# Spectral mixing and a gated FFN on one core: inverse tables made on chip, the first batch's mixing on idle PSUM banks, its first norm without memory

## The chip, the cores and the metric

One core of one Trainium2 chip. The time is the device time of one launch in microseconds (us); lower is better. The kernel before takes 1032.24 us (median of 4 runs, 1030.58 to 1034.24).

## The reference, cut to what matters

```python
# x: (8, 3008, 256) fp32; filters: (1505, 256) real and imaginary part
X = np.fft.rfft(x, axis=1)
y = np.fft.irfft(X * (filt_r + 1j * filt_i)[None], n=3008, axis=1)      # mixing along the sequence
t = y.reshape(24064, 256)
tn = t / np.sqrt(np.mean(t * t, -1, keepdims=True) + 1e-6) * rms_g     # RMS norm
g = tn @ w_gate                                                        # 256 -> 1536
out = (g / (1 + np.exp(-g)) * (tn @ w_val)) @ w_out                    # 1536 -> 256
```

## The kernel before

The transform of length 3008 = 47 x 64 is done as matrix products, a batch at a time: a 64-point stage (`a_unit`, table `wa`), a trip through memory that turns the data (`z_store`, `t2_load`), then in 16 units a 47-point stage (`b_unit`, table `wb`), the filter product and the inverse 47-point stage (`bi_unit`, table `wi`), a second trip through memory (`g_store`, `t4_load`), and the inverse 64-point stage (`n_unit`, table `wai`), which already gives the transposed tile that the norm and the FFN want. Every batch has six token tiles, and a tile has 12 FFN slots (`gv`: gate, value, product; `down`: the last product). While the FFN of one batch runs, the mixing and norms of the next are spread over its slots. The first batch has no FFN to hide behind: its mixing is the opening of the program, and this change is about that opening.

```python
psG, psV: 2 PSUM banks each (gate, value)   psO: 2 (output)   psM: 2 (all of mixing and norm)

def a_unit(b, i):                       # 12 a batch
    ps = psM.tile([P, 512], FP32, tag="mx")
    nc.tensor.matmul(ps, wa, x[c][:, 2*r:2*r+2, :])
    nc.scalar.activation(out=t1[c][:, 2*r:2*r+2, :], in_=ps, func=AXT.Copy)
def b_unit(b, i):                       # 16 a batch
    ps = psM.tile([P, 2, D], FP32, tag="mx", name="psb")
    for u in range(2):
        nc.tensor.matmul(ps[:, u, :], wb[:, k, :], t2[k // KC][:, k % KC, :])
    nc.vector.tensor_tensor(out=s1, in0=ps, in1=fr[c][:, r:r+2, :], op=ALU.mult)
    nc.vector.tensor_tensor(out=s2, in0=ps, in1=fi[c][:, r:r+2, :], op=ALU.mult)
def bi_unit(b, i):
    ps = psM.tile([P, 2, D], FP32, tag="mx", name="psi")
    ...                                 # four matmuls with wi on s1, s2; ACT evicts to t3
def t4_load(b, c):                      # four DMAs a chunk, all on the sync queue
    nc.sync.dma_start(t[p0:p0+32], g_d[b, :, r0:r0+XC, :])
def q_unit(b, m):                       # sum of squares by matmul with ones, then rho = u ** -0.5 on POOL
def rho_move(b, m):                     # rho to memory and back, spread over all partitions
    nc.sync.dma_start(r_d[b, m], rho)
    nc.sync.dma_start(rb, r_d[b, m]....partition_broadcast(P))
def xn_unit(b, m):
    nc.gpsimd.tensor_tensor(out=xn, in0=y, in1=rb, op=ALU.mult)
# ... the opening
x_load(0, c) for 4 chunks               # POOL queue
wa, wb, wi[:, 0:8]                      # sync queue
8 fills of the filter tiles on DVE;  filter and FFN weight loads on the POOL queue
12 x a_unit(0), z_store(0);  wi[:, 8:16];  t2_load(0, 0..2);  wi[:, 16:32];  wai, gains
f_dup(0);  16 x (b_unit(0, i), bi_unit(0, i - 1)), f_dup and g_store between
t4_load(0);  norm and rho_move of tiles 0 and 1;  xn_unit(0, 0), xn_unit(0, 1)
x_load(1, c)                            # POOL queue, behind both xn_units
# ... the loop: slot by slot; batch 1's a_units in slots 0 to 11
```

`f_dup(c)` copies a filter tile's lower half to its upper half, one copy on DVE and one on ACT. The line numbers (L...) of the profiles are those of each kernel's own file, so the same step has other numbers before and after.

Of the kernel before, what the change touches and what calls it, by code (L numbers as in the profile page):

```python
# [38 lines left out]
def _make_tables():  # L39
# [19 lines left out]
    wi = np.zeros((P, K2, 2, P))  # L59
    re, im = slice(0, N1), slice(SL, SL + N1)  # L60
    for k2 in range(K2):
        for s in range(48):

            if s < 24:
                k = k2 + 64 * s
                sign, q = 1.0, s
            else:
                j = s - 23
                k = 64 * j - (k2 if k2 else 32)
                sign, q = -1.0, 32 + s - 24  # L70
                if j == 24 and k2:
                    continue
            th = 2 * np.pi * ((n1 * k) % N) / N
            c, sn = np.cos(th), np.sin(th)
            if k == 0 or k == NF - 1:
                sn = np.zeros(N1)
            if k2:
                wb[re, k2, q] = c
                wb[im, k2, q] = sign * sn
                wb[re, k2, HALF + q] = -sn  # L80
                wb[im, k2, HALF + q] = sign * c

                gr = (c, -sn)
                gi = (sign * sn, sign * c)
            else:
                src = re if s < 24 else im
                wb[src, k2, q] = c
                wb[src, k2, HALF + q] = -sn
                m = 1.0 if k in (0, NF - 1) else 2.0
                z = np.zeros(N1)  # L90
                g = (m * c, -m * sn)
                gr, gi = (g, (z, z)) if s < 24 else ((z, z), g)

            wi[q, k2, 0, re] = gr[0]
            wi[q, k2, 0, im] = gi[0]
            wi[HALF + q, k2, 0, re] = gr[1]
            wi[HALF + q, k2, 0, im] = gi[1]
            wi[q, k2, 1, re] = gr[1]
            wi[q, k2, 1, im] = gi[1]
            wi[HALF + q, k2, 1, re] = -gr[0]  # L100
            wi[HALF + q, k2, 1, im] = -gi[0]
    f = np.float16
    wi = wi * S_INV_B
    return (wa.astype(f), (wai * S_INV_A).astype(f), wb.astype(f), wi.astype(f))
# [3 lines left out]
def kernel(  # L108
# [13 lines left out]
    wa_np, wai_np, wb_np, wi_np = _make_tables()  # L122
# [3 lines left out]
    wi_d = nc.inline_tensor(wi_np, name="wi_t").ap()  # L126
# [8 lines left out]
    t1p = ctx.enter_context(tc.tile_pool(name="t1p", bufs=3))  # L135
# [17 lines left out]
    wai = glob.tile([P, P], FP16)  # L153
    wb = glob.tile([KR, K2, P], FP16)
# [25 lines left out]

    def a_unit(b, i):
        c, r = divmod(i, XC // 2)
        if r == 0:
            st[b]["t1"][c] = t1p.tile([P, XC, D], FP16, tag="t1", name="t1")
        ps = psM.tile([P, 512], FP32, tag="mx", name="psa")
        nc.tensor.matmul(ps, wa, st[b]["x"][c][:, 2 * r:2 * r + 2, :], start=True, stop=True)  # L186
        nc.scalar.activation(out=st[b]["t1"][c][:, 2 * r:2 * r + 2, :],
                             in_=ps.rearrange("p (a d) -> p a d", a=2), func=AXT.Copy)
# [14 lines left out]
    def b_unit(b, i):  # L203
        ps = psM.tile([P, 2, D], FP32, tag="mx", name="psb")
# [8 lines left out]
        nc.vector.tensor_tensor(out=s2, in0=ps, in1=fi[c][:, r:r + 2, :], op=ALU.mult)  # L213
        st[b]["s"][i] = (s1, s2)

    def bi_unit(b, i):
        s12 = st[b]["s"].pop(i)
        ps = psM.tile([P, 2, D], FP32, tag="mx", name="psi")
# [13 lines left out]
    def t4_load(b, c):  # L232
        t = t4p.tile([P, XC, D], FP16, tag="t4", name="t4")
        for h in range(2):
            for ri in range(2):
                p0 = h * 64 + ri * 32
                r0 = ri * SL + h * H + c * XC
                nc.sync.dma_start(t[p0:p0 + 32, :, :], g_d[b, :, r0:r0 + XC, :])
        st[b]["t4"][c] = t
# [44 lines left out]
    def rho_move(b, m):  # L284
# [4 lines left out]
        st[b]["u"][m] = rb  # L289

# [88 lines left out]

    with tc.manual_schedule():  # L380
# [3 lines left out]
        nc.sync.dma_start(wb, wb_d)  # L384
        nc.sync.dma_start(wi[:, 0:KC], wi_d[:, 0:KC])
# [3 lines left out]
        nc.vector.memset(ones, 1.0)  # L389
        nc.vector.memset(mhalf, -0.5)  # L390
# [8 lines left out]
        for c in range(NXC):  # L399
            for i in range(3):  # L400
                a_unit(0, 3 * c + i)
            z_store(0, c)
        nc.sync.dma_start(wi[:, KC:2 * KC], wi_d[:, KC:2 * KC])
        for c in range(3):
            t2_load(0, c)
        for c in range(2, NC):
            nc.sync.dma_start(wi[:, c * KC:(c + 1) * KC], wi_d[:, c * KC:(c + 1) * KC])
        nc.sync.dma_start(wai, wai_d)
        for dh in range(2):
            nc.sync.dma_start(gsb[:, dh:dh + 1], moe_rms_g[ds(dh * P, P)].unsqueeze(-1))  # L410
# [14 lines left out]
        for m in range(2):  # L425
            n_unit(0, m, 0)
            n_unit(0, m, 1)
            q_unit(0, m)
            rho_move(0, m)
        for m in range(2):  # L430
            xn_unit(0, m)
# [15 lines left out]

        for m in range(2, 6):
            norm_plan(0, m, (m - 2) * 10)
        for b in range(1, B):  # L450
            t = (b - 1) * 72
            for i in range(12):
                at(t + i, a_unit, b, i)
                if i % 3 == 2:
                    at(t + i + 1, z_store, b, i // 3)
            for c in range(4):
                at(t + 13 + c if c < 3 else t + 24, t2_load, b, c)
            for i in range(16):
                s0 = t + 16 + 2 * i
# [7 lines left out]
            for c in range(4):  # L467
                at(t + 53, t4_load, b, c)
# [45 lines left out]
```

## Time and profile before

| stretch of the opening | us |
|---|---|
| start to the first filter product | 46.5 |
| first product to last inverse eviction (the B stage) | 37.7 |
| last eviction to the first gate matmul | 19.2 |
| first gate matmul, at | 103.4 |
| PE waiting for batch 1's x after that | 6.0 |

First the page: the span in 40 slices of 26 us, the busy share of TensorE and of the DMA engines in tenths.

```profile
PE   2162789999999999999999999999999999999997
DMA  9973556324743356323643356324743343322111
```

TensorE is busy from the fifth slice on; before that it is not. The opening is the only place where much can be won. The timeline of the opening in the kernel before (columns: start, duration, engine, line, operation, output<-inputs, shapes, count; in brackets how long the engine had been idle and what ended that):

```profile
23.72 1.70 SPq L196 DMA_DIRECT2D z_tmp<-t_235  x4
33.64 0.32 SPq L200 DMA_DIRECT2D t_250<-z_tmp  x1
45.88 1.01 PE L207 MATMUL psb<-t_250,wb 96*128 96x256 f16 x4 [22.83 <-DMA t_250<-z_tmp]
46.51 0.69 DVE L212 TENSOR_TENSOR s_266<-psb,fr_113 128x512 f16<-128x512 f32 x1 [25.82 <-PE psb L207]
...
80.40 0.59 PE L207 MATMUL psb<-t_328,wb 96*128 96x256 f16 x2 [0.68 <-ACT t_458 L226]
81.02 0.69 DVE L212 TENSOR_TENSOR s_477<-psb,fr_116 128x512 f16<-128x512 f32 x1 [0.83 <-PE psb L207]
...
83.61 0.59 ACT L226 ACTIVATE t_486<-psi 96x512 f16<-96x512 f32 x1 [1.10 <-PE psi L221]
90.30 1.04 PE L252 MATMUL psn<-wai,t_495 128*128 128x128 f16 x8 [6.72 <-DMA t_500<-g_tmp]
100.51 2.85 POOL L299 TENSOR_TENSOR xn<-y,rb 128x1024 f16<-128x1024 f32 x1 [2.51 <-DMA rb<-r_tmp]
103.41 1.01 PE L319 MATMUL pg<-xn,wg 128*128 128x512 f16 x2 [6.70 <-POOL xn L299]
111.72 0.59 PE L186 MATMUL psa<-xc,wa 128*128 128x512 f16 x1 [6.01 <-DMA xc<-in_x_dram]
```

Read it from above. The turned data of the first stage (t2) lands only at 45.9 us; the last store that it depends on went out at 23.7. In the B stage PE waits for an ACT eviction before it may start the next `psb`, and DVE then waits for that `psb`: two PSUM banks pass between the two kinds of product. The scale goes through memory before POOL may multiply at 100.5. And six of the microseconds after the first gate are a wait for x.

The matmuls of one `psi` start 0.21 us apart in the B stage, and 0.11 us apart in the loop: TensorE works at half its later speed in the B stage.

### The profile page before, as it was taken

The page shows a single profiled execution, that of the slowest core. Times are in us where ns is not written, and L with a number is a line of the kernel's source. Part 1 is how long each engine was busy: PE and PEld are TensorE (multiplying, and loading weights), DVE is VectorE, ACT ScalarE, POOL GpSimd, SP SyncE. Part 2 cuts the span into 40 slices and gives each one's busy share as a digit, 9 for nine tenths or more (in the row PEclk, how much of TensorE's full clock was granted, in tenths as well). Part 3 has the DMA queues.
Part 4 walks back from the last instruction along what each step waited for, and adds up shares of the span by engine and source line. Part 5 has one row for each costly group of instructions (what it writes and reads, how often), then busy time and mean ns, then how long its engine had stood idle before and what let it go on. Part 6 is the DMA issues. An engine that isn't in the chain of part 4 may idle for free.

```text
span 1031.0 us, 17242 instructions
## 1 busy us (share of the span) xinstructions
PE 931.7 (90%) x6240; PEld 565.0 (55%) x6240; DVE 591.7 (57%) x966; ACT 597.5 (58%) x1046; POOL 246.0 (24%) x218
## 2 busy tenths in 40 slices
PE   2162789999999999999999999999999999999997
PEld 0031356655666556655666566655666556656654
DVE  5161257744775457744775467644775467645553
ACT  3043555557655766557655766557655766556543
POOL 5501423113410333013410333013410332023200
PEclk9999999999999999999999999999999999999999
DMA  9973556324743356323643356324743343322111
GB/s 210 192 149 99 112 117 130 91 80 109 156 91 99 79 130 146 99 74 102 159 92 99 78 132 147 102 71 106 156 96 105 80 118 92 99 69 60 41 42 39
DMA packets 95941, 109.51 MB, mean 106 GB/s; under 512 B 17352, under 2 KB 70088, under 8 KB 95568
## 3 DMA queue, kind: packets, MB, share of 16 engines
q1 hardware_dynamic: 85744, 90.64, 33.9%
q0 software_dynamic: 10112, 17.77, 11.2%
q8 instruction: 49, 0.80, 0.3%
q14 instruction: 36, 0.29, 0.1%
HBM read 73.14 MB, written 49.91 MB: 119 GB/s over the span
## 4 chain that ended last, share of the span: by engine, by line
PE 76%; DMA 9%; DVE 5%; ACT 5%; issue 3%; SPq 1%; POOL 0%; ACTq 0%; DVEq 0%; POOLq 0%
PE pg L319 21%; PE pv L319 20%; PE psi L221 6%; PE psb L207 3%; ACT sq L261 2%; PE psn L252 1%; PE psa L186 1%; DMA fi_120<-in_filt_i_dram 1%; DMA fi_119<-in_filt_i_dram 1%; PE psq L269 1%; ACT y L259 1%; DVE hh L324 1%; DMA rb<-r_tmp 1%; DMA fr_114<-in_filt_r_dram 1%; SPq L196 1%
## 5 line engine op out<-in xcount | busy, mean ns | idle before, releaser
L324 DVE TENSOR_TENSOR hh<-pv,sg 128x512 f16<-128x512 f32 (+1 forms) x576 | 390.9, 679 | 363.8 <-ACT sg L323 217.0
L323 ACT ACTIVATE sg<-pg 128x512 f16<-128x512 f32 (+1 forms) x576 | 340.6, 591 | 313.5 <-PE pg L319 311.6
L319 PE MATMUL pg<-xn,wg 128*128 128x512 f16 (+1 forms) x1152 | 340.4, 377 | 6.7 <-POOL xn L299 6.7
L319 PE MATMUL pv<-xn,wv 128*128 128x512 f16 (+1 forms) x1152 | 339.4, 376 | 0.0
L336 PEld LDWEIGHTS <-hh 128*128 128x128 f16 (+1 forms) x2304 | 221.9, 98 | 108.9 <-issue 32.7
L299 POOL TENSOR_TENSOR xn<-y,rb 128x1024 f16<-128x1024 f32 (+1 forms) x48 | 132.5, 2760 | 316.6 <-DMA rb<-r_tmp 233.2
L319 PEld LDWEIGHTS <-wv 128*128 128x128 f16 x1152 | 113.2, 98 | 132.3 <-issue 2.5
L281 POOL TENSOR_TENSOR rho<-u,mhalf 128x4 f32<-128x4 f32 x48 | 48.7, 1015 | 388.1 <-DVE u L279 366.4
L319 PEld LDWEIGHTS <-wg 128*128 128x128 f16 x1152 | 105.9, 98 | 29.0 <-issue 7.3
L221 PEld LDWEIGHTS <-wi 128*128 128x128 f16 x512 | 51.5, 103 | 47.4 <-issue 4.5
L259 ACT ACTIVATE y<-psn,gsb 128x512 f32<-128x512 f32 (+1 forms) x96 | 65.8, 685 | 14.2 <-DMA t_500<-g_tmp 6.7
L186 PE MATMUL psa<-xc,wa 128*128 128x512 f16 x96 | 39.0, 412 | 23.6 <-DMA xc<-in_x_dram 16.6
L207 PEld LDWEIGHTS <-wb 96*128 96x128 f16 x256 | 23.7, 101 | 65.4 <-issue 40.6
L261 ACT ACTIVATE sq<-psn 128x512 f16<-128x512 f32 (+1 forms) x96 | 56.8, 592 | 0.0
L178 POOL DMA_DIRECT2D xc<-in_x_dram x64 | 34.7, 559 | 0.8 <-POOLq L498 0.8
L186 PEld LDWEIGHTS <-wa 128*128 128x128 f16 x96 | 9.5, 100 | 33.8 <-issue 20.4
L269 PEld LDWEIGHTS <-sq 128*128 128x128 f16 (+1 forms) x384 | 17.4, 97 | 14.4 <-ACT sq L261 4.1
L207 PE MATMUL psb<-t_250,wb 96*128 96x256 f16 x8 | 2.3, 410 | 22.9 <-DMA t_250<-z_tmp 22.8
L269 PE MATMUL psq<-ones,sq 128*128 128x1 f16 (+1 forms) x384 | 17.6, 165 | 3.4 <-ACT sq L261 3.4
L279 DVE TENSOR_SCALAR u<-psq 128x4 f32<-128x4 f32 (+2 forms) x56 | 7.8, 152 | 15.2 <-PE psq L269 14.3
L212 DVE TENSOR_TENSOR s_266<-psb,fr_113 128x512 f16<-128x512 f32 x1 | 0.7, 692 | 25.8 <-PE psb L207 25.8
L226 ACT ACTIVATE t_284<-psi 96x512 f16<-96x512 f32 x2 | 1.2, 594 | 19.7 <-PE psi L221 19.7
(949 smaller groups left out, 1144.3 us busy)
## 6 DMA issues: line engine op xcount, KB each, us to landing
rb<-r_tmp SPq DMA_DIRECT2D x48, 256.0 KB, 4.0
xc<-in_x_dram POOLq DMA_DIRECT2D x56, 192.0 KB, 6.0
wi<-wi_t SPq DMA_DIRECT2D x4, 512.0 KB, 13.3
xc<-in_x_dram POOLq DMA_DIRECT2D x8, 160.0 KB, 7.0
wb<-wb_t SPq DMA_DIRECT2D x1, 768.0 KB, 5.6
wg<-in_moe_w_gate_dram POOLq DMA_DIRECT2D x4, 192.0 KB, 13.3
wv<-in_moe_w_val_dram POOLq DMA_DIRECT2D x4, 192.0 KB, 12.2
wo<-in_moe_w_out_dram POOLq DMA_DIRECT2D x4, 192.0 KB, 13.0
```

The costliest lines, as they stand in the source:

```text
L186: nc.tensor.matmul(ps, wa, st[b]["x"][c][:, 2 * r:2 * r + 2, :], start=True, stop=True)
L207: nc.tensor.matmul(ps[:, u, :], wb[:, k, :], st[b]["t2"][k // KC][:, k % KC, :], start=True, stop=True)
L221: nc.tensor.matmul(ps[:, u, :], wi[:, 2 * i + u, q, :], s12[q][:, u, :], start=(q == 0), stop=(q == 1))
L259: nc.scalar.activation(out=y[:, dh, 0:w], in_=ps[:, 0:w], func=AXT.Identity, scale=gsb[:, dh:dh + 1])
L261: nc.scalar.activation(out=st[b]["sq"][m][:, dh, 0:w], in_=ps[:, 0:w], func=AXT.Square)
L269: nc.tensor.matmul(ps[0:w, q:q + 1], sq[:, dh, q * P:q * P + w], ones, start=(dh == 0), stop=(dh == 1))
L281: nc.gpsimd.tensor_tensor(out=rho, in0=u, in1=mhalf, op=ALU.pow)
L299: nc.gpsimd.tensor_tensor(out=xv[:, :, 0:nq], in0=yv[:, :, 0:nq], in1=rv[:, 0:nq].unsqueeze(1).to_broadcast([P, 2, nq, P]), op=ALU.mult)
L319: nc.tensor.matmul(ps[:, 0:w], wt[:, dt_, ts(jt, P)], xn[:, dt_, 0:w], start=(dt_ == 0), stop=(dt_ == 1))
L323: nc.scalar.activation(out=sg[:, 0:w], in_=pg[:, 0:w], func=AXT.Silu)
L324: nc.vector.tensor_tensor(out=hh[:, 0:w], in0=pv[:, 0:w], in1=sg[:, 0:w], op=ALU.mult)
L336: nc.tensor.matmul(po[s4 // 2][0:w, s4 % 2, :], hh[:, s4 * P:s4 * P + w], wo[:, jt, :], start=(jt == 0 and s4 % 2 == 0), stop=(jt == JT - ...
```

## The change: its intent, and the diff

The inverse tables are transposes of the forward ones (31 of the 32), so 2 MB of table loads become 64 KB and 31 small transposes on TensorE. The gate and value banks are idle in the opening, so the first batch's mixing may use six banks; half of its second products go over ACT to POOL. Tile 0's scale is spread over the partitions by matmuls, without memory. Cut to its core:

```diff
-        nc.sync.dma_start(wb, wb_d)
-        nc.sync.dma_start(wi[:, 0:KC], wi_d[:, 0:KC])
+        nc.sync.dma_start(ident, id_d)
         for c in range(NC):
             nc.vector.memset(fr[c][0:HALF], 0.0)
             nc.vector.memset(fi[c][0:HALF], 0.0)
+            ...
+            for i in range(3):
+                a_unit(0, 3 * c + i)          # 3 banks; odd ones evicted by DVE, the others by ACT
+            z_store(0, c)
 ...
+        nc.sync.dma_start(wb, wb_d)
         for c in range(3):
             t2_load(0, c)
-        for c in range(2, NC):
-            nc.sync.dma_start(wi[:, c * KC:(c + 1) * KC], wi_d[:, c * KC:(c + 1) * KC])
+        nc.sync.dma_start(wi[:, 0], wi0_d)
         nc.sync.dma_start(wai, wai_d)
+        for g in range(8):
+            wi_group(g)          # 4 transposes; ACT evicts one half of wi, DVE the other in two passes
     def b_unit(b, i):
-        ps = psM.tile([P, 2, D], FP32, tag="mx", name="psb")
+        ps = bank(0 if b else i % 2, "psb")...         # psM and psG in turn
 ...
-        nc.vector.tensor_tensor(out=s2, in0=ps, in1=fi[c][:, r:r + 2, :], op=ALU.mult)
+        if b == 0 and i % 2:
+            nc.scalar.activation(out=v, in_=ps, func=AXT.Copy)
+            nc.gpsimd.tensor_tensor(out=s2, in0=v, in1=fi[c][:, r:r + 2, :], op=ALU.mult)
+        else:
+            nc.vector.tensor_tensor(out=s2, in0=ps, in1=fi[c][:, r:r + 2, :], op=ALU.mult)
     def bi_unit(b, i):
-        ps = psM.tile([P, 2, D], FP32, tag="mx", name="psi")
+        ps = bank(0 if b else 2, "psi")...             # psV
     def t4_load(b, c):
-                nc.sync.dma_start(t[p0:p0 + 32, :, :], g_d[b, :, r0:r0 + XC, :])
+                (nc.scalar if b == 0 and h else nc.sync).dma_start(...)
-        for m in range(2):
-            n_unit(0, m, 0); n_unit(0, m, 1); q_unit(0, m); rho_move(0, m)
-        for m in range(2):
-            xn_unit(0, m)
+        norm_first()             # tile 0: rho as two fp16 parts, 8 matmuls with ident, 2 DVE products
+        n_unit(0, 1, 0); n_unit(0, 1, 1); q_unit(0, 1); rho_move(0, 1)
         for c in range(NXC):
             x_load(1, c)
+        at(4, xn_unit, 0, 1)
+            a0, b0, bs = (6, 22, 7) if b == 1 else (0, 16, 8)      # batch 1 six slots later, packed
-                at(t + 53, t4_load, b, c)
+                at(t + 54, t4_load, b, c)
```

Further, the t1 pool goes from three buffers to two (the first batch uses the four t4 buffers instead).

More of the change, by code (lines that the diff above doesn't have):

```diff
@@ L58, in _make_tables @@
     wb = np.zeros((KR, K2, P))
-    wi = np.zeros((P, K2, 2, P))
+    wi = np.zeros((P, 1, 2, P))
     re, im = slice(0, N1), slice(SL, SL + N1)
@@ L81, in _make_tables @@
                 wb[im, k2, HALF + q] = sign * c
-                gr = (c, -sn)
-                gi = (sign * sn, sign * c)
             else:
@@ L92, in _make_tables @@
                 gr, gi = (g, (z, z)) if s < 24 else ((z, z), g)
-            wi[q, k2, 0, re] = gr[0]
-            wi[q, k2, 0, im] = gi[0]
-            wi[HALF + q, k2, 0, re] = gr[1]
-            wi[HALF + q, k2, 0, im] = gi[1]
-            wi[q, k2, 1, re] = gr[1]
-            wi[q, k2, 1, im] = gi[1]
-            wi[HALF + q, k2, 1, re] = -gr[0]
-            wi[HALF + q, k2, 1, im] = -gi[0]
+                for qq, cols in ((re, 0), (im, 1)):
+                    wi[q, 0, 0, qq] = (gr, gi)[cols][0]
+                    wi[HALF + q, 0, 0, qq] = (gr, gi)[cols][1]
+                    wi[q, 0, 1, qq] = (gr, gi)[cols][1]
+                    wi[HALF + q, 0, 1, qq] = -(gr, gi)[cols][0]
     f = np.float16
-    wi = wi * S_INV_B
-    return (wa.astype(f), (wai * S_INV_A).astype(f), wb.astype(f), wi.astype(f))
+    wi0 = wi[:, 0] * S_INV_B
+    return wa.astype(f), (wai * S_INV_A).astype(f), wb.astype(f), wi0.astype(f), np.eye(P).astype(f)
 @with_exitstack
@@ L120 @@
     nc = tc.nc
-    wa_np, wai_np, wb_np, wi_np = _make_tables()
+    wa_np, wai_np, wb_np, wi0_np, id_np = _make_tables()
     wa_d = nc.inline_tensor(wa_np, name="wa_t").ap()
@@ L125 @@
     wb_d = nc.inline_tensor(wb_np, name="wb_t").ap()
-    wi_d = nc.inline_tensor(wi_np, name="wi_t").ap()
+    wi0_d = nc.inline_tensor(wi0_np, name="wi0_t").ap()
+    id_d = nc.inline_tensor(id_np, name="id_t").ap()
     z_d = nc.dram_tensor("z_tmp", (B, K2, KR, D), FP16, kind="Internal").ap()
@@ L134 @@
     xp = ctx.enter_context(tc.tile_pool(name="xp", bufs=4))
-    t1p = ctx.enter_context(tc.tile_pool(name="t1p", bufs=3))
+    t1p = ctx.enter_context(tc.tile_pool(name="t1p", bufs=2))
     t2p = ctx.enter_context(tc.tile_pool(name="t2p", bufs=3))
@@ L153 @@
     wai = glob.tile([P, P], FP16)
+    ident = glob.tile([P, P], FP16)
     wb = glob.tile([KR, K2, P], FP16)
@@ L179, in x_load, with bank @@
         st[b]["x"][c] = t
+    def bank(i, name):
+        pool, tag = ((psM, "mx"), (psG, "pg"), (psV, "pv"))[i]
+        return pool.tile([P, 512], FP32, tag=tag, name=name)
     def a_unit(b, i):
@@ L183, in a_unit @@
         if r == 0:
-            st[b]["t1"][c] = t1p.tile([P, XC, D], FP16, tag="t1", name="t1")
-        ps = psM.tile([P, 512], FP32, tag="mx", name="psa")
+            st[b]["t1"][c] = (t1p.tile([P, XC, D], FP16, tag="t1", name="t1") if b else
+                              t4p.tile([P, XC, D], FP16, tag="t4", name="t1"))
+        ps = bank(0 if b else i % 3, "psa")
+        dst = st[b]["t1"][c][:, 2 * r:2 * r + 2, :]
         nc.tensor.matmul(ps, wa, st[b]["x"][c][:, 2 * r:2 * r + 2, :], start=True, stop=True)
-        nc.scalar.activation(out=st[b]["t1"][c][:, 2 * r:2 * r + 2, :],
-                             in_=ps.rearrange("p (a d) -> p a d", a=2), func=AXT.Copy)
+        src = ps.rearrange("p (a d) -> p a d", a=2)
+        if b == 0 and i % 2:
+            nc.vector.tensor_copy(out=dst, in_=src)
+        else:
+            nc.scalar.activation(out=dst, in_=src, func=AXT.Copy)
     def z_store(b, c):
@@ L203, in b_unit @@
     def b_unit(b, i):
-        ps = psM.tile([P, 2, D], FP32, tag="mx", name="psb")
+        ps = bank(0 if b else i % 2, "psb").rearrange("p (a d) -> p a d", a=2)
         for u in range(2):
@@ L212, in b_unit @@
         nc.vector.tensor_tensor(out=s1, in0=ps, in1=fr[c][:, r:r + 2, :], op=ALU.mult)
-        nc.vector.tensor_tensor(out=s2, in0=ps, in1=fi[c][:, r:r + 2, :], op=ALU.mult)
+        if b == 0 and i % 2:
+            v = yp.tile([P, 2, 512], FP32, tag="y", name="v")
+            v = v[:, 0, :].rearrange("p (a d) -> p a d", a=2)
+            nc.scalar.activation(out=v, in_=ps, func=AXT.Copy)
+            nc.gpsimd.tensor_tensor(out=s2, in0=v, in1=fi[c][:, r:r + 2, :], op=ALU.mult)
+        else:
+            nc.vector.tensor_tensor(out=s2, in0=ps, in1=fi[c][:, r:r + 2, :], op=ALU.mult)
         st[b]["s"][i] = (s1, s2)
@@ L217, in bi_unit @@
         s12 = st[b]["s"].pop(i)
-        ps = psM.tile([P, 2, D], FP32, tag="mx", name="psi")
+        ps = bank(0 if b else 2, "psi").rearrange("p (a d) -> p a d", a=2)
         for u in range(2):
@@ L237, in t4_load @@
                 r0 = ri * SL + h * H + c * XC
-                nc.sync.dma_start(t[p0:p0 + 32, :, :], g_d[b, :, r0:r0 + XC, :])
+                (nc.scalar if b == 0 and h else nc.sync).dma_start(t[p0:p0 + 32, :, :],
+                                                                   g_d[b, :, r0:r0 + XC, :])
         st[b]["t4"][c] = t
@@ L289, in rho_move, with norm_first @@
         st[b]["u"][m] = rb
+    def norm_first():
+        y = yp.tile([P, 2, 512], FP32, tag="y", name="y")
+        sq = sqp.tile([P, 2, 512], FP16, tag="sq", name="sq")
+        for dh in range(2):
+            ps = bank(1 + dh, "psn")
+            for q in range(4):
+                nc.tensor.matmul(ps[:, ts(q, P)], st[0]["t4"][q // XC][:, q % XC, ds(dh * P, P)], wai,
+                                 start=True, stop=True)
+            nc.scalar.activation(out=sq[:, dh, :], in_=ps, func=AXT.Square)
+            nc.vector.tensor_scalar(out=y[:, dh, :], in0=ps, scalar1=gsb[:, dh:dh + 1], scalar2=None,
+                                    op0=ALU.mult)
+        st[0]["sq"][0] = sq
+        q_unit(0, 0)
+        rho = st[0]["u"].pop(0)
+        hl = up.tile([P, 2, 4], FP16, tag="hl", name="hl")
+        nc.vector.tensor_copy(out=hl[:, 0, :], in_=rho)
+        nc.vector.tensor_tensor(out=hl[:, 1, :], in0=rho, in1=hl[:, 0, :], op=ALU.subtract)
+        ps = bank(1, "psr")
+        for q in range(4):
+            for e in range(2):
+                nc.tensor.matmul(ps[:, ts(q, P)], hl[:, e, q:q + 1].to_broadcast([P, P]), ident,
+                                 start=(e == 0), stop=(e == 1))
+        xn = xnp.tile([P, 2, 512], FP16, tag="xn", name="xn")
+        for dh in range(2):
+            nc.vector.tensor_tensor(out=xn[:, dh, :], in0=ps, in1=y[:, dh, :], op=ALU.mult)
+        st[0]["xn"][0] = xn
     def xn_unit(b, m):
@@ L378, in f_dup, with wi_group @@
         nc.scalar.activation(out=fi[c][HALF:P], in_=fi[c][0:HALF], func=AXT.Copy)
+    def wi_group(g):
+        ps = bank(1 + g % 2, "pst").rearrange("p (a d) -> p a d", a=4)
+        lo = 1 if g == 0 else 0
+        for a in range(lo, 4):
+            nc.tensor.matmul(ps[:, a, :], wb[:, 4 * g + a, :], ident[0:KR, :], start=True, stop=True)
+        k = slice(4 * g + lo, 4 * g + 4)
+        nc.scalar.activation(out=wi[:, k, 0, :], in_=ps[:, lo:4, :], func=AXT.Copy, scale=S_INV_B)
+        for p0, sign in ((0, 1.0), (HALF, -1.0)):
+            nc.vector.tensor_scalar(out=wi[p0:p0 + HALF, k, 1, :],
+                                    in0=ps[HALF - p0:P - p0, lo:4, :], scalar1=sign * S_INV_B,
+                                    scalar2=None, op0=ALU.mult)
     with tc.manual_schedule():
@@ L388 @@
             nc.vector.memset(fi[c][0:HALF], 0.0)
-        nc.vector.memset(ones, 1.0)
-        nc.vector.memset(mhalf, -0.5)
+            if c == 0:
+                nc.vector.memset(ones, 1.0)
+                nc.vector.memset(mhalf, -0.5)
+            for i in range(3):
+                a_unit(0, 3 * c + i)
+            z_store(0, c)
         for c in range(NC):
@@ L398 @@
                                 moe_w_out.rearrange("(jt p) d -> p jt d", p=P)[:, ts(q, 3), :])
-        for c in range(NXC):
-            for i in range(3):
-                a_unit(0, 3 * c + i)
-            z_store(0, c)
-        nc.sync.dma_start(wi[:, KC:2 * KC], wi_d[:, KC:2 * KC])
+        nc.sync.dma_start(wb, wb_d)
         for c in range(3):
             t2_load(0, c)
-        for c in range(2, NC):
-            nc.sync.dma_start(wi[:, c * KC:(c + 1) * KC], wi_d[:, c * KC:(c + 1) * KC])
+        nc.sync.dma_start(wi[:, 0], wi0_d)
         nc.sync.dma_start(wai, wai_d)
-        for dh in range(2):
-            nc.sync.dma_start(gsb[:, dh:dh + 1], moe_rms_g[ds(dh * P, P)].unsqueeze(-1))
+        with nc.allow_non_contiguous_dma(reason="one gain a partition"):
+            nc.sync.dma_start(gsb, moe_rms_g.rearrange("(a p) -> p a", p=P))
+        for g in range(8):
+            wi_group(g)
         f_dup(0)
@@ L424 @@
             t4_load(0, c)
-        for m in range(2):
-            n_unit(0, m, 0)
-            n_unit(0, m, 1)
-            q_unit(0, m)
-            rho_move(0, m)
-        for m in range(2):
-            xn_unit(0, m)
+        norm_first()
+        n_unit(0, 1, 0)
+        n_unit(0, 1, 1)
+        q_unit(0, 1)
+        rho_move(0, 1)
         for c in range(NXC):
@@ L451 @@
             t = (b - 1) * 72
+            a0, b0, bs = (6, 22, 7) if b == 1 else (0, 16, 8)
             for i in range(12):
-                at(t + i, a_unit, b, i)
+                at(t + a0 + i, a_unit, b, i)
                 if i % 3 == 2:
-                    at(t + i + 1, z_store, b, i // 3)
+                    at(t + a0 + i + 1, z_store, b, i // 3)
             for c in range(4):
-                at(t + 13 + c if c < 3 else t + 24, t2_load, b, c)
+                at(t + b0 - 3 + c if c < 3 else t + b0 + 8, t2_load, b, c)
             for i in range(16):
-                s0 = t + 16 + 2 * i
+                s0 = t + b0 + bs * i // 4
                 at(s0, b_unit, b, i)
```

## The prediction

> **What bounds it now.** From about 112 us the kernel is TensorE-bound: the stage windows show PE busy 95 to 100% of each 50 us until the tail. Before that PE is mostly idle, and the timeline cuts the opening into: x and filter loads with the first mixing, 0 to 46 us (the 16 DMA engines are 97 to 100% busy from 10 us); the B stage of the first batch (filter products and inverse), 46.5 to 84.2 us; store, reload, norm through memory, first gate matmul at 103.4 us; then PE stands still 6.0 us (105.7 to 111.7) for batch 1's x, the largest PE wait in the loop. Only these parts can change much; the loop's work is the same.
>
> **Opening to B.** 2 MB of inverse tables leave the DMA queues, but B need not start earlier. DVE now mixes the eight fills (1.76 us each, 2.14 us apart) with six evictions, which wait for x, so I work out that the last forward eviction still ends near 25 us (now 23.7). Then z stores land in 6 to 8 us under filter traffic, wb comes behind them (estimate 34 us), and eight table groups need two DVE passes each, about 0.61 us apart as the s1/s2 pairs are: 9.5 us, then the filter duplicate 1.22 us. First product near 46 to 47 us, as before. The binding input moves from t2 to wb plus DVE.
>
> **B stage.** Four banks for psb and two for psi remove the bank wait, and DVE drops from 0.61+0.69 per unit to three products per pair. But an odd unit is a chain: psb to product 0.64, DVE 0.69, ACT copy 0.6, POOL product, psi. Different engines' readers of one bank take turns (the Trainium skill, "PSUM — Partial Sum Buffer", Terms, says they must not meet; the build's waits put the ACT copy after the DVE product), and POOL has no PSUM port there. POOL's multiply costs 2.87 us at 1024 columns and 0.51 at 128, so about 1.5 us at 512, of the size of the two-input rate in "GPSIMD Engine Reference", section 3.1. PE is in order and the next odd psb stands behind this psi, so a pair takes about 4.5 us; before it was 4.3, or 4.9 with the duplicates, which now hide. Eight pairs: about 37 us against 37.7. Gain 0 to 4 us.
>
> **Norm.** The memory round trip of rho (95.0 to 100.5) and the 2.85 us POOL multiply become eight small matmuls and two DVE products. Yet PE must still finish tile 1's norms before the gate, and ACT now issues half the reloads, the later ones waiting on DMA lanes. I estimate 4 us saved.
>
> **x stall.** x loads are issued before the POOL multiplies and batch 1's mixing starts six slots later: 6 us saved. A dip of the granted clock near 140 us (0.66) costs about 1.7 us and may stay.
>
> **Loop.** Two t1 buffers should do: stores land in 2 to 3 us, chunks come 4.6 us apart. Neutral, plus or minus 2.
>
> **Sum.** 0.5 + 1 + 4 + 6, about 12 us: 1020 us, range 1010 to 1028. Faster by over 2% 0.17, within 2% 0.80, slower 0.03.
>
> **Shown right or wrong by:** first product at 46 to 47 us; pair period 4.5 us with psi waiting on POOL; first gate matmul near 98 to 99 us; no 6 us PE wait on x; PE loop waits for t2 unchanged (about 1 to 2 us a batch).
>
> **Would make it wrong:** tables landing well before 34 us; POOL held by weight DMA issues, which stand ahead of its products, delaying B; a faster POOL multiply (contiguous operands); t4 loads one slot later starving the norms in every batch.

## More of the kernel before

The experiments ran on several chips, each beside its own runs of the kernel before, so across experiments the ratio to before is the number to compare. Each ratio carries its own interval, mostly of 0.3% to either side, so two ratios from different chips are told apart only when their intervals do not overlap; a step is therefore also read inside the profiled runs, from which all microsecond positions come.

## The result, and the profile after

1029.45 us (median of 4 runs, 1028.90 to 1030.52) against 1032.24: ratio 0.9973, 95% interval 0.9953 to 0.9994. (A ratio is the mean time of one kernel's runs over the mean of the other's from the same rounds, so not quite the ratio of the medians.) So the change wins a quarter of a per cent where 1.2 was predicted, and the time lies outside the range of 1010 to 1028.

The same places in the timeline of the changed kernel:

```profile
23.44 1.70 SPq L204 DMA_DIRECT2D z_tmp<-t_197  x4
25.18 0.46 SPq L458 DMA_DIRECT2D wb<-wb_t  x1
33.17 0.32 SPq L208 DMA_DIRECT2D t_250<-z_tmp  x1
38.95 1.78 PE L428 MATMUL pst<-ident,wb 96*128 96x128 f16 x15 [24.26 <-DMA wb<-wb_t]
40.02 11.03 DVE L432 TENSOR_SCALAR wi<-pst 64x384 f16<-64x384 f32 x16 [16.64 <-ACT wi L430]
46.49 1.01 PE L215 MATMUL psb<-t_250,wb 96*128 96x256 f16 x4 [0.42 <-DMA t_250<-z_tmp]
52.29 0.69 DVE L220 TENSOR_TENSOR s_327<-psb,fr_114 128x512 f16<-128x512 f32 x1
55.27 0.39 PE L235 MATMUL psi<-s_327,wi 128*128 128x256 f16 x1 [7.77 <-DMA wi<-wi_t]
...
86.50 0.59 ACT L240 ACTIVATE t_563<-psi 96x512 f16<-96x512 f32 x1 [1.74 <-PE psi L235]
93.85 1.01 PE L313 MATMUL psn<-wai,t_572 128*128 128x128 f16 x8 [7.38 <-DMA t_577<-g_tmp]
95.22 1.08 ACT L315 ACTIVATE sq<-psn 128x512 f16<-128x512 f32 x2 [8.12 <-DMA t_582<-g_tmp]
102.86 1.01 PE L362 MATMUL pg<-xn,wg 128*128 128x512 f16 x2
```

The t2 data lands at 46.5 us, as before. But now DVE is still making tables: wb lands at 38.9, the sixteen table passes last from 40.0 to 51.1, a filter duplicate follows, and the first product comes at 52.3, 5.8 us later than before. The DMA issues of the two kernels say how late wb is (KB, then us from issue to landing; the first line is before, the next fence is the change):

```profile
wb<-wb_t SPq DMA_DIRECT2D x1, 768.0 KB, 5.6
```

```profile
wb<-wb_t SPq DMA_DIRECT2D x1, 768.0 KB, 13.7
...
wi<-wi_t SPq DMA_DIRECT2D x1, 64.0 KB, 15.2
```

Stretch by stretch. Mixing and FFN of the loop can be set beside each other because each of the 48 output tiles leaves by one ACT eviction, whose time the timeline gives.

| stretch (profiled runs) | before | after | difference |
|---|---|---|---|
| start to first filter product | 46.51 | 52.29 | +5.8 |
| B stage, first product to last eviction | 37.69 | 34.80 | -2.9 |
| last eviction to first gate | 19.21 | 15.77 | -3.4 |
| first gate to eviction of batch 0's last tile | 132.01 | 126.46 | -5.6 |
| from there to the last tile's eviction | 789.49 | 791.89 | +2.4 |
| tail | 6.09 | 5.89 | -0.2 |
| span | 1031.0 | 1027.1 | -3.9 |

The first gate matmul, the sum of the first three rows, moves from 103.4 only to 102.9. Nearly all that is left is the wait for x, which is gone from the list of PE's waits in the loop. Part of the loop's +2.4 us is a longer wait and a lower clock near 832 us (a wait of 2.84 us for t2, where the kernel before waits 1.74 at the same place). Windows of the changed kernel there (PE busy, granted clock, DMA share, GB/s):

```profile
825.00:830.00 5.00, 4.27 (x25) 1.00 0.53 129
830.00:835.00 5.00, 2.84 (x12) 0.74 0.20 47
835.00:840.00 5.00, 5.00 (x38) 0.92 0.94 269
```

The kernel before has such a dip once in the loop of its profiled run, near 142 us, the change twice.

One unit of the changed B stage, odd and so by way of ACT and POOL:

```profile
78.19 0.63 PE L215 MATMUL psb<-t_393,wb 96*128 96x256 f16 x2
78.86 0.69 DVE L220 TENSOR_TENSOR s_522<-psb,fr_117 128x512 f16<-128x512 f32 x1 [1.47 <-PE psb L215]
79.65 0.60 ACT L224 ACTIVATE v<-psb 128x512 f32<-128x512 f32 x1 [0.62 <-DVE s_522 L220]
80.32 1.26 POOL L225 TENSOR_TENSOR s_523<-v,fi_121 128x512 f16<-128x512 f32 x1 [2.77 <-ACT v L224]
81.64 0.37 PE L235 MATMUL psi<-s_523,wi 128*128 128x256 f16 x1 [1.32 <-POOL s_523 L225]
```

Each link starts when the one before ends. From one such `psi` to the next is 4.0 us (77.60 to 81.64), and DVE, which was to be relieved, is idle for 2.1 us of it (1.47 before this product and 0.59 before the next). The chain, not an engine, sets the pace: PE stands idle for 1.32 us until POOL is done, and the next pair's `psb` comes only behind this `psi` (at 82.23 us), as the program has it.

### The profile page after: what moved, and what is told of

It reads as the page before. It is cut to its first block, busy times and chain, and to the rows that moved or that the text cites. A ratio compares the mean times of both kernels' runs of the same rounds, so it can differ in the third digit from the quotient of the medians.

```text
span 1027.1 us, 17356 instructions
## 1 busy us (share of the span) xinstructions
PE 934.9 (91%) x6279; PEld 569.6 (55%) x6279; DVE 604.7 (59%) x986; ACT 601.4 (59%) x1054; POOL 252.8 (25%) x225
## 4 chain that ended last, share of the span: by engine, by line
PE 75%; DMA 8%; DVE 5%; ACT 5%; issue 3%; SPq 2%; POOL 1%; ACTq 0%; DVEq 0%; POOLq 0%
PE pg L362 21%; PE pv L362 20%; PE psi L235 5%; PE psb L215 3%; SPq L204 2%; PE psn L267 2%; DMA wi<-wi_t 1%; PE psa L191 1%; ACT sq L276 1%; ACT y L274 1%; PE psq L284 1%; DMA z_tmp<-t_197 1%; DVE hh L367 1%; SPq L208 1%; DMA t_10462<-z_tmp 0%
## 5 line engine op out<-in xcount | busy, mean ns | idle before, releaser
L342 POOL TENSOR_TENSOR xn<-y,rb 128x1024 f16<-128x1024 f32 (+1 forms) x47 | 129.8, 2761 | 307.7 <-DMA rb<-r_tmp 238.3
L296 POOL TENSOR_TENSOR rho<-u,mhalf 128x4 f32<-128x4 f32 x48 | 48.7, 1015 | 365.1 <-DVE u L294 348.9
L235 PEld LDWEIGHTS <-wi 128*128 128x128 f16 x512 | 51.8, 103 | 55.8 <-issue 12.2
L215 PEld LDWEIGHTS <-wb 96*128 96x128 f16 x256 | 24.7, 104 | 35.9 <-issue 14.6
L428 PE MATMUL pst<-ident,wb 96*128 96x128 f16 x31 | 4.2, 310 | 27.2 <-DMA wb<-wb_t 24.3
L432 DVE TENSOR_SCALAR wi<-pst 64x512 f16<-64x512 f32 (+1 forms) x16 | 10.7, 671 | 16.9 <-ACT wi L430 16.6
L430 ACT ACTIVATE wi<-pst 128x512 f16<-128x512 f32 (+1 forms) x8 | 4.4, 584 | 27.4 <-PE pst L428 27.4
L428 PEld LDWEIGHTS <-wb 96*128 96x128 f16 x31 | 2.9, 138 | 29.1 <-DMA wb<-wb_t 25.2
## 6 DMA issues: line engine op xcount, KB each, us to landing
wb<-wb_t SPq DMA_DIRECT2D x1, 768.0 KB, 13.7
```

The costliest lines, as they stand in the source:

```text
L215: nc.tensor.matmul(ps[:, u, :], wb[:, k, :], st[b]["t2"][k // KC][:, k % KC, :], start=True, stop=True)
L235: nc.tensor.matmul(ps[:, u, :], wi[:, 2 * i + u, q, :], s12[q][:, u, :], start=(q == 0), stop=(q == 1))
L296: nc.gpsimd.tensor_tensor(out=rho, in0=u, in1=mhalf, op=ALU.pow)
L342: nc.gpsimd.tensor_tensor(out=xv[:, :, 0:nq], in0=yv[:, :, 0:nq], in1=rv[:, 0:nq].unsqueeze(1).to_broadcast([P, 2, nq, P]), op=ALU.mult)
```

## The experiments

Theory 1: the waits that the change takes away are real gains (x, norm, banks), and it gives them back at the front, because its tables are made on the critical path (wb late, then sixteen DVE passes), and in the B stage, because the way over ACT and POOL is a chain that is longer than DVE's own work. Theory 2: the DMA engines are full in the opening, so the same bytes in any order give the same start; and DVE was the limit of the B stage, so only the split could help. All the kernels of the experiments gave correct results.

| kernel | ratio to before (95% interval) | first product | B stage | to gate | first gate |
|---|---|---|---|---|---|
| the change | 0.9973 (0.9953 to 0.9994) | 52.3 | 34.8 | 15.8 | 102.9 |
| wb first | 0.9929 (0.9896 to 0.9962) | 46.7 | 38.8 | 15.6 | 101.2 |
| tables loaded | 0.9945 (0.9911 to 0.9979) | 50.2 | 34.6 | 16.0 | 100.8 |
| DVE alone | 0.9844 (0.9808 to 0.9880) | 53.2 | 25.4 | 15.6 | 94.2 |
| reload on sync | 0.9959 (0.9925 to 0.9992) | 55.6 | 34.6 | 14.5 | 104.8 |
| before, batch 1 later | 0.9988 (0.9950 to 1.0025) | 49.5 | 37.7 | 19.5 | 106.6 |
| before, six banks | 0.9895 (0.9858 to 0.9931) | 46.9 | 27.6 | 19.3 | 93.9 |
| wb and small table first | 0.9874 (0.9850 to 0.9898) | 47.6 | 34.6 | 15.5 | 97.8 |
| combined | 0.9764 (0.9735 to 0.9794) | 48.7 | 25.4 | 14.3 | 88.4 |
| combined, later B in the loop | 0.9850 (0.9822 to 0.9879) | 45.2 | 25.1 | 14.2 | 84.6 |
| the change, later B in the loop | 1.0043 (1.0011 to 1.0074) | 54.4 | 34.5 | 15.9 | 104.8 |
| combined, fills apart | 0.9795 (0.9764 to 0.9825) | 39.2 | 28.2 | 14.3 | 81.7 |
| all | 0.9844 (0.9815 to 0.9874) | 40.5 | 27.2 | 12.2 | 79.9 |
| combined, fills and norm moved | 0.9768 (0.9744 to 0.9792) | 40.5 | 27.4 | 12.0 | 80.0 |
| the change, norm by memory | 1.0022 (0.9995 to 1.0049) | 53.1 | 34.1 | 20.4 | 107.6 |
| combined again | 0.9789 (0.9767 to 0.9811) | 48.7 | 25.1 | 14.2 | 88.0 |

(us, each from that kernel's profiled run; "to gate" is from the last inverse eviction to the first gate matmul. The front of one program moves by some 3 us from run to run: five kernels share the change's front, and their first products come between 52.3 and 55.6 us; "DVE alone" at 53.2 and "reload on sync" at 55.6 ran on the same chip.)

### wb first

```diff
         nc.sync.dma_start(wa, wa_d)
+        nc.sync.dma_start(wb, wb_d)
         nc.sync.dma_start(ident, id_d)
 ...
-        nc.sync.dma_start(wb, wb_d)
```

> The changed kernel with one load moved: wb goes out right after wa, not behind the z stores. Theory 1 (the inverse tables are made late because wb lands late: issued at 25.2 us, landed at 38.9): the table groups now run as soon as DVE has done the last forward eviction, 23.5 to 35 us, the first product of the B stage moves from 52.3 us to 42 to 46 us, and the time falls by 6 to 10 us, to about 1021. Theory 2 (the DMA engines are full from 10 to 60 us, so any order of the same bytes gives the same start): x lands later by about 3 us, the first product stays at 50 to 53 us, and the time stays within 2 us of 1029.5.

1026.86 us (1024.70 to 1027.47), ratio 0.9929. The first product moved to 46.7 us, most of the way to the 42 to 46 that theory 1 expected, but the ratio fell by only 0.44%, some 4.5 us, where 6 to 10 were expected, and its interval overlaps the change's. One reason is in theory 2: with wb ahead of it x lands later, the forward mixing starts at 9.7 us instead of 6.0 and its last eviction ends at 27.1 instead of 23.4. The timeline of this run shows the other:

```profile
46.72 0.69 DVE L220 TENSOR_TENSOR s<-psb,fr 128x512 f16<-128x512 f32 x1 [7.46 <-PE psb L215]
...
54.73 1.04 PE L235 MATMUL psi<-s,wi 128*128 128x256 f16 x4 [7.62 <-DMA wi<-wi_t]
```

The one table that is still loaded, 64 KB, is issued behind the t2 loads, into the other traffic, and lands 16.8 us after its issue; the first inverse product cannot start without it. In the change this wait was hidden behind the late first product: its B stage takes 34.8 us with the wait and 34.6 without it (next run).

### wb and the small table first

```diff
+        nc.sync.dma_start(wb, wb_d)
         nc.sync.dma_start(ident, id_d)
+        nc.sync.dma_start(wi[:, 0], wi0_d)
 ...
-        nc.sync.dma_start(wb, wb_d)
-        nc.sync.dma_start(wi[:, 0], wi0_d)
```

> The changed kernel with wb and the one loaded inverse table (64 KB) both right after wa. In the run with wb alone moved, the first inverse matmul still waited for that small table until 54.7 us, though the first product came at 46.7. Theory 1 (that table, last in a full queue, held the stage): first psi at 48 to 50 us, end of the B stage at 80 to 83 us instead of 87.1 (85.5 with wb alone), the time 5 to 8 us under the change, about 1022 to 1024. Rival (the queues are full, the wait moves to t2 or the filters): end of the stage at 85 us or later, no gain over the run with wb alone.

1022.39 us (1021.26 to 1024.85), ratio 0.9874: a whole per cent better than the change, by the places of two loads. The timeline of this run:

```profile
47.01 1.01 PE L215 MATMUL psb<-t,wb 96*128 96x256 f16 x4 [14.25 <-DMA t<-z_tmp]
48.47 1.30 PE L235 MATMUL psi<-s,wi 128*128 128x256 f16 x4 [0.45 <-DVE s L220]
...
81.67 0.59 ACT L240 ACTIVATE t<-psi 96x512 f16<-96x512 f32 x1 [1.74 <-PE psi L235]
```

wb now lands in 5.7 us, the tables are ready at 37.7, `psi` starts at 48.5 and the B stage ends at 82.3. Theory 2's full queues are not the answer at this point. But the start is now where t2 lets it be (PE waits 14.3 us for t2), so it is no earlier than before the change. The first gate comes at 97.8 us, 5.1 us before the change's; the ratio fell by about 10 us, on another chip, and what of that lies outside the opening is not traced.

### Tables loaded as before

The edit puts back the loads of `wi` in their old places and takes away `wi_group`. It also puts wb back right after wa, so it is to be set beside the two runs above, which load wb there too, more than beside the change.

> The changed kernel with its inverse tables loaded by DMA as before (2 MB, same places in the queue), all else kept. Theory 1: the first product comes at 46 to 47 us as in the kernel before, 5 to 6 us earlier than the change has it, and the time falls to about 1024. Theory 2: 2 MB more in full queues delay everything; the first product is at 52 us or later and the time is the same or worse than 1029.5.

1029.01 us (1027.58 to 1029.70), ratio 0.9945. The first product came at 50.2 us, between what the two theories expected: earlier than the change's but not at 46 to 47. Better than the change by 0.3% of ratio, inside the intervals. So 2 MB of loads with wb early are no worse than tables made from a late wb, and worse than tables made from an early one (the run above: 0.9874, first product 2.6 us earlier).

### Both products on DVE

```diff
-        if b == 0 and i % 2:
-            v = yp.tile(...)
-            nc.scalar.activation(out=v, in_=ps, func=AXT.Copy)
-            nc.gpsimd.tensor_tensor(out=s2, in0=v, in1=fi[c][:, r:r + 2, :], op=ALU.mult)
-        else:
-            nc.vector.tensor_tensor(out=s2, in0=ps, in1=fi[c][:, r:r + 2, :], op=ALU.mult)
+        nc.vector.tensor_tensor(out=s2, in0=ps, in1=fi[c][:, r:r + 2, :], op=ALU.mult)
```

> The changed kernel with both products of every unit on DVE again (no ACT copy, no POOL product), the six banks kept. Theory 1 (the route DVE, ACT, POOL, psi is a chain of 4.1 to 4.4 us a pair, and PE in order cannot pass it): without it the stage is bound by DVE, 32 products 0.61 us apart and three duplicates, 23 to 27 us against 34.8, and the time falls by 8 to 11 us to about 1020. Rival (relieving DVE was needed, the banks alone give little): the stage stays at 34 us or more and the time at 1029 or above.

1017.82 us (1016.51 to 1020.02), ratio 0.9844. The B stage falls from 34.8 to 25.4 us:

```profile
53.16 0.69 DVE L220 TENSOR_TENSOR s<-psb,fr 128x512 f16<-128x512 f32 x1
53.77 0.68 DVE L221 TENSOR_TENSOR s<-psb,fi 128x512 f16<-128x512 f32 x1
...
77.98 0.59 ACT L234 ACTIVATE t<-psi 96x512 f16<-96x512 f32 x1 [0.55 <-PE psi L229]
```

The products now start 0.61 us apart; 32 of them and three duplicates of 1.22 us make about 23 us of DVE work, so DVE is the limit, at a shorter time. Theory 1's range for the stage held. Relieving DVE by the chain cost 9.4 us.

### The kernel before with six banks

The `bank` helper and its two uses in `b_unit` and `bi_unit`, both products on DVE as they were, in the kernel before.

> The kernel before with one part of the change alone: the first batch's B stage on six PSUM banks, both products on DVE. Theory 1 (two shared banks were the limit, DVE the next one): the stage from first product to last eviction falls from 37.7 us to 24 to 27 us and the time by 10 to 13 us, ratio 0.988 to 0.990. Rival (DVE is the limit already and only the split to ACT and POOL can shorten the stage): the stage stays above 33 us.

1024.83 us (1020.36 to 1026.53), ratio 0.9895. The B stage, from its first product to its last eviction:

```profile
46.95 0.69 DVE L216 TENSOR_TENSOR s<-psb,fr 128x512 f16<-128x512 f32 x1 [26.50 <-PE psb L211]
...
73.93 0.59 ACT L230 ACTIVATE t<-psi 96x512 f16<-96x512 f32 x1 [0.63 <-PE psi L225]
```

It takes 27.6 us, 0.6 more than theory 1's range, whose ratio held; the rival fell. These few lines, taken alone, win about four times what the whole change wins.

### The kernel before with batch 1 later

x loads ahead of the second scaling, batch 1's `a0, b0, bs = (6, 22, 7)`, `t4_load` in slot 54.

> The kernel before with one part of the change alone: batch 1's x loads are issued ahead of the second scaling, its forward mixing starts six slots later and its B stage is packed into 7/4 slot a unit. Theory 1 (the gain that the change shows is the 6.0 us PE wait for x, nearly alone): the first gate stays at 103.4 us, the wait of 6 us on x is gone, and the time falls by 5 to 6 us, to about 0.995 of before: more than the whole change gained. Rival (that wait only moves to the later z or t2 waits): less than 2 us faster.

1035.70 us (1030.02 to 1036.73), ratio 0.9988 (0.9950 to 1.0025): theory 1 missed, and the rival's mark (less than 2 us faster) was met. The wait for x is gone and the stretch from first gate to batch 0's last tile falls from 132.0 to 128.4 us, less than the 6.0 us, as PE now waits 5.6 us for batch 1's t2 instead of 2.2. The gate itself was 3.2 us later in this run, in a part that the edit does not touch, and the clock dipped three times in the loop. The run shows that most of the x wait can move into the next one; it does not give this part's worth inside the change, where that t2 wait was 3.1 us and the same stretch fell by 5.6.

### Reloads on the sync queue

> The changed kernel with all 16 reload DMAs of the first batch on the sync queue again. Theory 1 (ACT is held by its own DMA issues, which wait for lanes, until 95.2 us, and two queues mix the first chunk with the second): first norm matmul about 3.6 us after the issue starts instead of 4.4, the first square 1.3 us after it instead of waiting for ACT; 1.5 to 2 us faster. Rival (splitting halves the issue time and helps): 1 to 3 us slower.

1029.68 us (1027.85 to 1031.08), ratio 0.9959, within the interval of the change: the time shows neither theory. In the stretch that the edit touches, 15.8 us fell to 14.5; wb landed 3 us later in this run, which hides it. The timeline of this run, against the lines at 93.85 and 95.22 above:

```profile
96.25 1.01 PE L312 MATMUL psn<-wai,t 128*128 128x128 f16 x8 [6.63 <-DMA t<-g_tmp]
96.87 1.08 ACT L314 ACTIVATE sq<-psn 128x512 f16<-128x512 f32 x2 [6.62 <-PE psn L312]
```

The first square follows the matmul by 0.62 us; in the change by 1.37, as ACT was busy with its own DMA issues, whose last ones wait for earlier ones to land. And the first matmul came 3.7 us after the first reload's issue (92.59) instead of 4.4 (89.45 to 93.85). The Trainium skill, "DMA: Bandwidth & Descriptors", section "Issuing engines are not separate DMA queues", says that a second issuing engine saves only the sequencer's issue time; here it did save that (the 16 issues took 5.7 us, and 7.3 from one queue), and cost more.

### The norm by memory again

The change with tile 0 normed as tile 1 is.

> The changed kernel with one part undone: tile 0's scale goes through memory again, as before, with x loads still ahead of tile 1's scaling. Expected from the traces (last eviction of the B stage to the first gate: 19.2 us before, 15.8 us in the change): the gate 3 to 4 us later than the change's, and 3 to 4 us slower, about 1033. Rival (ACT, held by its reload issues, hides the round trip): less than 1.5 us slower.

1035.28 us (1032.57 to 1036.59), ratio 1.0022: against the change's 0.9973, on another chip, that is 0.5%, 5 us, and the stretch to the gate is 20.4 us instead of 15.8. The norm step was worth what the traces said, and a little more.

### Combined

wb and small table first, both products on DVE, all reloads on sync.

> The changed kernel with the three repairs together: wb and the small table first, both products on DVE, all reloads on the sync queue. Theory 1 (the three costs lie one after the other in the opening and add): first product at 46 to 47 us, B stage 25 us, gate at 87 to 89 us against 102.9; the time 14 to 17 us under the change, about 1013 to 1016. Rival (they share one hidden limit, the DMA queues, so only the largest counts): no better than the run with DVE alone, 1018.

1011.37 us (1009.25 to 1013.20), ratio 0.9764; run again on another chip, 1010.79 us and 0.9789. The costs lie one after the other and add: gate at 88.4 us, 14.5 us before the change's, where the three parts alone gave 5.1 and 8.7 us at the gate and 1.3 in the last stretch. The profiled run is 15.7 us shorter than the change's, so the loop gave none of it back.

> The combined kernel again, as the measure beside the kernel with the fills apart on one chip: gate near 88 us, ratio to before 0.975 to 0.98. If the loop gives back what the opening gains, both show the same time here.

### Later B stages in the loop

```diff
-            a0, b0, bs = (6, 22, 7) if b == 1 else (0, 16, 8)
+            a0, b0, bs = (6, 24, 6) if b == 1 else (0, 18, 7)
-                at(t + b0 - 3 + c if c < 3 else t + b0 + 8, t2_load, b, c)
+                at(t + b0 - 5 + c if c < 3 else t + b0 + 8, t2_load, b, c)
```

> The combined kernel (tables first, both products on DVE, reloads on the sync queue) with every later batch's B stage two slots later and packed closer, its t2 loads left where they were. In all runs so far PE waits 0.8 to 3 us a batch for t2, and a wait of about 2.5 us or more is mostly followed by 3 us at half clock. Theory: the seven waits (12 us in the combined run) shrink to under 3 us together and the clock dips in the loop go; 8 to 12 us under the combined kernel, about 1001. Rival (the packed B stage makes DVE or PSUM wait instead): within 3 us of it.

> The changed kernel with the same later, packed B stage in the later batches and nothing else. It asks whether the loop's waits for t2 are worth the same there: expected 8 to 12 us under the change, about 1019; if the change's own packing (7/4 slot a unit in batch 1, two t1 buffers) had cost the loop something that this does not touch, less than 5 us.

Both missed, the wrong way: 1017.07 us (0.9850) against the combined kernel's 0.9764, and 1036.54 us (1.0043) against the change's 0.9973. The waits for t2 and the clock dips in the loop did go, as expected; yet from the eviction of batch 0's last tile to that of the very last the runs took 799 and 801 us instead of 791 and 792. PE's waits of the second kernel from 112 us on:

```profile
PE po L379 <- DVE o L386: 5.2, 8, 1.0
PE psb L215 <- ACT sq L276: 4.8, 8, 0.8
PE psb L215 <- ACT t L240: 4.8, 7, 0.7
PE psb L215 <- DVE s L227: 2.6, 12, 0.2
```

Packed closer, the units wait for PSUM evictions on ACT and DVE: seven waits of 0.8 to 3.3 us, and some smaller ones, became some forty small ones. Between 250 and 990 us PE's idle time rose from 14.5 to 20.0 us in the second kernel; the rest of the loss is not resolved here. What looks like a cheap wait in the loop is also slack that others use.

### Fills apart, and everything together

The eight fills go ahead of the forward mixing and all its evictions to ACT (as before the change). "All" adds tile 1's norm in the loop's first slots and the later B stages; the last kernel is "all" without the later B stages.

> The combined kernel with the eight fills ahead of the forward mixing on DVE and all twelve forward evictions on ACT, as the kernel before had them, with the change's buffers and banks. Theory (DVE's fills between its evictions hold the last z store to 23.4 us and so t2): the last forward eviction ends at 15 to 18 us, t2 lands near 36 to 40 us, the first product comes at 37 to 41 us instead of 48.7, and the time falls 7 to 10 us under the combined kernel. Rival (t2 is bound by the bytes in the full DMA queues): t2 lands at 45 us or later and the gain is under 3 us.

> Everything together: the combined kernel, the fills apart, the later B stage, and tile 1's norm put into the first slots of the loop so that the first gate does not wait for it. Theory: the first gate moves from 88.4 us to 76 to 82 us and the loop loses its t2 waits; 990 to 998. It settles whether the parts add; if the waits only move, above 1001.

> The combined kernel with the fills apart and tile 1's norm moved into the first slots of the loop, the loop's own B stages left as the change has them. Theory (an earlier gate is worth its full time once the loop is left alone): gate near 79 to 81 us, 8 us before the combined kernel's, and 6 to 9 us faster than the combined kernel run beside it, about 1004. Rival (the loop gives it back: its waits for t2 are set by the loop's own DMA traffic and the clock dips that follow them): within 3 us of the combined kernel.

The front of the kernel with the fills apart:

```profile
30.39 1.48 SPq L205 DMA_DIRECT2D t<-z_tmp  x3
...
38.59 1.01 PE L212 MATMUL psb<-t,wb 96*128 96x256 f16 x4 [14.51 <-DMA t<-z_tmp]
```

With the fills apart the last forward eviction ends at 16.6 us, the first t2 load goes out at 30.4 us instead of 38.9, and the first product comes at 39.2: DVE's fills between its evictions had held the front, so the bytes alone were not the limit there. The theory's front held and the rival's fell. The gate moves to 81.7 (the B stage grew from 25.4 to 28.2 us, so 6.8 of the 9.5 us are left there), but the time was 1011.02 us (0.9795), no better than the combined kernel, where 7 to 10 us were expected; in this profiled run four waits in the loop were followed by clock dips. The later B stages spoil "all" (1016.28 us, 0.9844, where 990 to 998 was expected) as they spoiled the others. Side by side on one chip with five rounds, fills and norm moved took 1008.83 us (1008.04 to 1009.16) and the combined kernel 1010.79 (1010.06 to 1011.97): of 8.0 us at the gate 2.0 reach the end. The theory (6 to 9 us) missed and the rival (within 3 us) held. Between the first tile's eviction and the second's the faster opening loses 3.6 us again: batch 1's wait for t2 is 5.9 us there and 3.6 in the combined kernel. The best version is 2.3% faster than the kernel before.

## Why the prediction was wrong

- **The step that failed: "Opening to B ... First product near 46 to 47 us, as before."** It came at 52.3 us, and so the first gate at 102.9 instead of 98 to 99. The prediction named the binding input rightly, "wb plus DVE", but mis-sized it: t2 landed at 46.5, in time, and DVE made the tables until 51.1. Of the terms, "wb comes behind them (estimate 34 us)" was wrong by 5 us: wb landed at 38.9, 13.7 us after its issue at 25.2 behind the z stores, into DMA engines whose busy share in the trace was 1.01 from 10 to 40 us; issued right after wa the same load takes 5.7 to 6.4 us. "Eight table groups need two DVE passes each, about 0.61 us apart ... 9.5 us" was 11.0 us, 0.69 us a pass. With wb and the small table moved, the first product does come at 47.6 and the time falls by a per cent. This term, 5.8 us later where 0.5 us earlier was counted, is 6.3 of the 7.6 us by which the profiled run missed the sum of 11.5 us.
- **The last eviction near 25 us** was right (z stores from 23.4 us), and so was its cause: in the combined kernel the first product comes 9.5 us earlier when fills and evictions are apart. The prediction used it to say that B would not start earlier, but did not ask what else would then be late.
- **The B stage** was right in mechanism: the chain through ACT and POOL, PE in order behind it, a gain of 0 to 4 us (2.9 measured), 4.0 us a pair where 4.5 were predicted. The size of one link was off: POOL's product took 1.26 us, not 1.5, when it ran alone, and 1.60 to 1.67 in the three units where the filter duplicates ran beside it. The prediction's estimate came from a multiply whose second operand is read in steps of 16 bytes; the Trainium skill, "GPSIMD Engine Reference", section 7, says that reading in steps over 8 bytes costs a kernel on that engine about half as much again, which the prediction overlooked. The trace agrees in sign: 2.80 ns a column there (2.87 us at 1024), 2.46 ns for the contiguous product.
- **The norm** was predicted at 4 us: 3.4 in the traces, 4.6 in the stretch and 5 us in the time by undoing it. That ACT's reload issues would hold it was right; they cost 1.3 us of the stretch.
- **The x stall** was right: 6.0 us gone, 5.6 of them left at the end of batch 0. In the kernel before, by itself, most of it went into the next wait. No run says why the gain stayed in the change and not there, so this hit is in part luck.
- **The loop** was put as neutral within 2 us; it was 2.4 us longer in the profiled run, with one more clock dip. The other kernels with the change's loop took 788.7 to 797.5 us over the same stretch and the one with six banks, which has the old loop, 792.8, so this term is mostly scatter. The two t1 buffers were not run alone. "PE loop waits for t2 unchanged" held but for two of them (3.1 against 2.2 us, 2.8 against 1.7).
- The sum, with the measured terms: +5.8 - 2.9 - 3.4 - 5.6 + 2.4 - 0.2 = -3.9 us against -12 predicted.

What stays open: why batch 1's t2 wait differs from 2.8 to 5.9 us between kernels with the change's slots for batch 1, and where the front's 3 us scatter comes from.

## What to carry to other kernels

When work is made on chip instead of loaded, its own input joins the critical path: place that one load first, and check the small load that is left over, too. Before handing part of an engine's work to another, write the new chain link by link for one item and compare its period with the engine's own; TensorE, which takes its matmuls in the order of the program here, does not pass a slow link (1.3 us idle in a pair). And when an opening gets shorter, look at once for the wait behind it: here a quarter of the last 8 us reached the end.

## What the Trainium skill lacked or had wrong

- "TensorE: Matmul & The Clock Gate", section "HAM oscillation — how this bites in real kernels", gives the rule "no PE-idle gaps >~3.4µs." (its next section tells of dips from short idles, without a length). Here shorter ones were enough: of 22 waits of 2.4 us or more in the loops of the seventeen profiled runs, 19 were followed by a granted clock of 0.5 (the two waits of 6.0 us for x are left out: one fell before the clock record shows full speed, the other before the record begins), and so were waits of 1.91, 2.00 and 2.22 us, two others between 1.9 and 2.4 were not, and no shorter one was. A dip took about 1.7 us of full-clock time or twice that (windows of 2 us, one minus the clock, summed).
- "GPSIMD Engine Reference", section 3.1, puts a two-input `tensor_tensor` at about 2.6 cycles an element, so an estimate of 1.1 us at 512 columns and 1.2 GHz (the prediction's 1.5 us was not that near to it); the runs show 1.26 us. Its contention with VectorE, which the page's table of specifications names without a number, may be what the 1.60 to 1.67 us beside the duplicates show; DVE's and ACT's duplicates ran together there, so no run separates them. Section 7's half as much again for steps over 8 bytes is too much for this multiply, one of whose two operands has such steps: 2.80 against 2.46 ns a column.
- "PSUM — Partial Sum Buffer", section "Terms", says that ScalarE and VectorE may not touch one bank at once. The build's waits keep them apart (ACT's copy starts 0.03 to 0.10 us after DVE's product ends, in every odd unit), so no run tests it; the page gives no cost for the turns; here they make two links of a chain of 4.0 us a pair.
- "DMA: Bandwidth & Descriptors", section "Issuing engines are not separate DMA queues", does not tell the other side of issuing from ScalarE: its compute waits behind its own DMA issues (the first square 1.37 us after its matmul instead of 0.62 without them).
